# Linear attention, MoE and a second MoE on one core: four of seven VectorE steps of the first three weight conversions given to GpSimd

## The chip, the cores and the metric

The kernel runs on one core of a Trainium2 chip. The metric is the device time of one execution in microseconds (us). Five engines work side by side, each through its own list of instructions in a fixed order: TensorE multiplies matrices, VectorE (DVE in the profile) and ScalarE (ACT) work elementwise, GpSimd (POOL) can do so too, and SyncE (SP) issues the DMA transfers. An instruction that waits for another engine holds up everything behind it in its own list.

## What is computed

```
kv  = einsum('bhsd,bhse->bhde', k, v)          # attention: 4 batches, 8 heads, 576 x 64
out = einsum('bhsd,bhde->bhse', q, kv)
x   = out / sqrt(mean(out**2) + 1e-6) * g_norm # -> 2304 tokens x 512
h   = x @ w_in                                 # first MoE, 512 -> 2048 -> 512, weights float64
x   = (h * clip(h + 3, 0, 6) / 6) @ w_out
for e in range(4):                             # second MoE, experts 512 -> 1024 -> 512
    y += p[:, e] * (relu(x @ w1[e]) @ w2[e])   # p: domain_probs, normalised
```

The weights `w_in` and `w_out` of the first MoE come as float64. They are read as pairs of 32-bit words and turned on the chip into a float32 value, which is then split into a high and a low part.

## The kernel before

The attention goes in eight half batches (4 batches, 4 heads at a time). For half batch i the program does: `att_load` (three DMAs for q, k, v); `att_q` (TensorE transposes q into `pq` and `kvp`, ScalarE copies it to `qT`, L217); `att_kv` (TensorE forms k'v in `kvp`, L227; ScalarE copies it to `qT` and to `kvbd`, L232 and L234); `att_out` (TensorE multiplies `qT` with `kvbd` into `po`, L247; ScalarE squares `po`, L253; VectorE sums the squares, L256); `att_rms` (ScalarE takes a root `s`, L277; VectorE makes `va`, `r0`, `ri`, L279 to L285, and scales `po` into `xt`, L269); `att_x` (TensorE transposes `xt` into `px`, L304; ScalarE and VectorE write its high and low parts, L314 and L315). The three banks of `po` are the same for every half batch, so the matmuls of the next one wait until L269 has read them.

Beside this run the conversions of the weights. The first MoE has 16 weight tiles of 128 hidden units; a tile is a half of `w_in` (h = 0) and a half of `w_out` (h = 1). Each half takes three steps on ScalarE (Abs of the high words into `x`, L144; a copy of the low words into `r`, L145; the high part of the result `w`, L160) and seven on VectorE: the clamp of `x` (L147), the shifts of `x` (L149), the bit operations into `a` and back into `x` (L153, L155), the multiplication and addition in `r` (L157, L158), and the subtraction that gives the low part (L162). `x` and `a` have one buffer each and `r` has two, so a half can't begin on `x` before the half ahead of it has multiplied. Raw words have three buffers.

`convert` is a generator; `pull` takes steps from it against a budget of ns. The order in which each engine's instructions stand is not that of the code, though: a scheduler settles it when the program is built, out of its own idea of when each is ready. It puts the conversions of tiles 0 to 2 among the instructions of the eight half batches. Tiles 0 to 2 here are the three with n = 0, 1, 2.

After the half batches TensorE works through the first MoE (`ff_in`, `ff_out`), and then the second.

Of the kernel before, what the change touches and what calls it, by code (L numbers as in the profile page):

```python
# [8 lines left out]
F32 = mybir.dt.float32  # L9
# [3 lines left out]
ALU = mybir.AluOpType  # L13
# [4 lines left out]
def kernel(  # L18
# [18 lines left out]
    nc = tc.nc  # L37
# [20 lines left out]
    TH = 384  # L58
    FP = NF2 // 2
    NW = 8  # L60
    NA = NW - 2
    LAG = 3
    RATE = (4200, 3000, 2600, 2900, 0)
# [53 lines left out]
    def load_raw():  # L117
        if not todo:
            return
        n, h = todo.pop(0)  # L120
        u, f = ftiles[n]
        g = sum(UNITS1[:u]) + f
        r = rawp.tile([P, KD * P, 2], U32, tag="raw", name="raw")
        if h == 0:
            nc.sync.dma_start(
                out=r.rearrange("p (c f) w -> p c (f w)", c=KD),
                in_=moe_w_in.bitcast(U32)[:, 2 * g * P:2 * (g + 1) * P].rearrange("(c p) f -> p c f", p=P))
        else:
            nc.sync.dma_start(
                out=r.rearrange("p e w -> p (e w)"), in_=moe_w_out.bitcast(U32)[g * P:(g + 1) * P, :])  # L130
        raw[n, h] = r

    def convert(n):

        u, f = ftiles[n]
        W[u, f] = w = wp.tile([P, 2, 2, KD * P], F32R, tag=f"w{(NA + n) % NW}", name="w")

        for h in range(2):
            lo, hi = raw[n, h][:, :, 0], raw[n, h][:, :, 1]
            x = cvp.tile([P, KD * P], U32, tag="x", name="x")  # L140
            a = cvp.tile([P, KD * P], U32, tag="a", name="a")
            r = cvp.tile([P, KD * P], F32, tag="r", bufs=2, name="r")
            xf = x.bitcast(F32)
            nc.scalar.activation(out=xf, in_=hi.bitcast(F32), func=AF.Abs)  # L144
            nc.scalar.activation(out=r, in_=lo, func=AF.Copy, scale=2.0 ** -52)  # L145
            yield 0
            nc.vector.tensor_scalar(  # L147
                out=xf, in0=xf, scalar1=2.0 ** -15, scalar2=122880.0, op0=ALU.max, op1=ALU.min)
            nc.vector.tensor_scalar(  # L149
                out=x, in0=x, scalar1=5, scalar2=2,  # L150
                op0=ALU.logical_shift_left, op1=ALU.logical_shift_right)
            yield 670
            nc.vector.scalar_tensor_tensor(  # L153
                out=a, in0=hi, scalar=0xC0000000, in1=x, op0=ALU.bitwise_and, op1=ALU.bitwise_or)
            nc.vector.tensor_scalar(out=x, in0=a, scalar1=0xFF800000, scalar2=None, op0=ALU.bitwise_and)  # L155
            yield 940
            nc.vector.tensor_tensor(out=r, in0=r, in1=xf, op=ALU.mult)  # L157
            nc.vector.tensor_tensor(out=r, in0=r, in1=a.bitcast(F32), op=ALU.add)  # L158
            yield 1200
            nc.scalar.activation(out=w[:, h, 0], in_=r, func=AF.Copy)  # L160
            yield 0
            nc.vector.tensor_tensor(out=w[:, h, 1], in0=r, in1=w[:, h, 0].bitcast(F32), op=ALU.subtract)  # L162
            load_raw()
            yield 600

# [242 lines left out]
    def pull(n):  # L408
        while cv[0] < len(ftiles):
            i = cv[0]  # L410
            u, f = ftiles[i]
            if cv[1] is None:
                if i >= NW and last[ftiles[i - NW]] > n - LAG:
                    return
                if u and start[u - 1, 0] > n:
                    return
                cv[1] = convert(i)
            urgent = start[u, f] <= n + 1
            if budget[0] <= 0 and not urgent:
                return  # L420
            try:
                budget[0] -= next(cv[1])
            except StopIteration:
                cv[0], cv[1] = i + 1, None

    firsts = convert(0)

    def conv(k):
# [3 lines left out]

    zero = wp.tile([P, DM], mybir.dt.bfloat16, tag=f"w{NW - 1}", name="zero")
    nc.vector.memset(zero, 0.0)
# [51 lines left out]
    for n in range(NI):  # L486
        step(n)
        if n == 4 * NB:
# [6 lines left out]
                out=prob, in0=dp, in1=psum_e.unsqueeze(2).to_broadcast([P, NTT, E]), op=ALU.mult)  # L495
# [32 lines left out]
    def load2(k):  # L528
        if k >= NQ:
            return  # L530
        _, e, j = quads[k]
        raw2[k] = r = wp.tile([P, 2, 2 * KD * P], F32, tag=f"w{(NA + len(ftiles) + k % 2) % NW}", name="raw2")
        f = 2 * j * P
# [31 lines left out]
    def convert_out(k):  # L565

        r = raw2.pop(k)[:, 1].rearrange("p (f d) -> p f d", f=2)
        wout[k] = w = wp.tile(
            [P, 2, 2, DM], F32R, tag=f"w{(NA + len(ftiles) + 2 + k % 2) % NW}", name="wout")
        for f in range(2):  # L570
# [106 lines left out]
    def quad(k):  # L677
# [3 lines left out]
        g2[k] = g = [  # L681
            wp.tile([P, 2, 2, TH], F32R, tag=f"w{(NA + len(ftiles) + 4 + 2 * (k % 2) + f) % NW}", name="g2")
            for f in range(2)]
# [112 lines left out]
```

## Time and profile before

| | before |
|---|---|
| median of 3 runs | 1229.06 us (1228.98 to 1230.06) |
| profiled execution | 1228.86 us, of which the span from first to last instruction 1227.0 us |
| TensorE (PE) busy | 1206.8 us, 98% of the span |
| VectorE busy | 771.0 us, 63% |
| ScalarE busy | 586.6 us, 48% |
| GpSimd busy | 1.6 us, 13 instructions |
| granted TensorE clock | 0.999 over the span |

The chain that ended last is 93% TensorE. Busy time of TensorE is a model and overlaps itself, so 98% says that little is idle and not that all of it is at its peak. What is idle lies in the first 90 us, where the eight half batches are.

### The profile page before, as it was taken

How to read it: one execution, taken by the hardware profiler on the slowest of the kernel's cores; microseconds unless marked ns; L12 is line 12 of the kernel's file. 1: busy time of each engine (PE TensorE's matmuls, PEld its weight loads, DVE VectorE, ACT ScalarE, POOL GpSimd, SP SyncE). 2: the span in 40 equal slices, each digit the busy share in tenths (PEclk: the TensorE clock that was granted, in tenths of full speed). 3: DMA queues.
4: the chain of work that ended last, by engine and by line, in shares of the span. 5: the costliest groups of instructions: out<-in, count | busy, mean ns of one | idle time of the engine just before them, and what ended most of it. 6: DMA issues, size and time to landing. Idle time of an engine off the chain costs nothing.

```text
span 1227.0 us, 17550 instructions
## 1 busy us (share of the span) xinstructions
PE 1206.8 (98%) x7069; PEld 1061.9 (87%) x7069; DVE 771.0 (63%) x1469; ACT 586.6 (48%) x1146; POOL 1.6 (0%) x13
## 2 busy tenths in 40 slices
PE   7899999999999999999999999999999999999998
PEld 5778888888888889999999989999999899999997
DVE  5989996673522645565656585656565856565653
ACT  6778453442422434444444554444444644444442
POOL 0000000000000000000000000000000000000000
PEclk9999999999999999999999999999999999999999
DMA  8812221110100002221122132211222221111101
GB/s 338 261 58 86 70 86 35 43 44 1 37 33 1 1 1 70 69 69 69 69 70 69 69 116 73 70 69 69 69 69 69 87 92 64 65 65 63 68 32 52
DMA packets 60833, 87.15 MB, mean 71 GB/s; under 512 B 5200, under 2 KB 37968, under 8 KB 60752
## 3 DMA queue, kind: packets, MB, share of 16 engines
q1 hardware_dynamic: 60592, 86.03, 20.5%
q8 instruction: 55, 0.90, 0.3%
q14 instruction: 26, 0.21, 0.0%
q10 hardware_dynamic: 160, 0.00, 0.0%
HBM read 81.30 MB, written 4.72 MB: 70 GB/s over the span
## 4 chain that ended last, share of the span: by engine, by line
PE 93%; DVE 3%; ACT 1%; DMA 1%; issue 0%; SPq 0%
PE po L637 32%; PE po L356 16%; PE qa L663 14%; PE qb L663 14%; PE ph L333 5%; PE ph L334 5%; PE ph L335 5%; PE po L247 1%; DMA raw<-in_moe_w_out_dram 1%; DVE acc L653 1%; DVE xl L315 1%; PE px L304 0%; DVE xt L269 0%; DMA qin<-in_q_dram 0%; DVE ssq L256 0%; ACT xh L314 0%
## 5 line engine op out<-in xcount | busy, mean ns | idle before, releaser
L637 PE MATMUL po<-wout,g 128*128 128x512 f32 x1728 | 402.1, 390 | 0.0
L637 PEld LDWEIGHTS po<-wout,g 128*128 128x128 f32 x1728 | 323.6, 188 | 65.4
L663 PE MATMUL qb<-xs,win 128*128 128x384 f32 x1008 | 203.3, 336 | 1.2 <-ACT us L704 1.2
L663 PE MATMUL qa<-xs,win 128*128 128x384 f32 x1008 | 203.0, 336 | 0.0
L356 PE MATMUL po<-gH,w 128*128 128x512 f32 (+1 forms) x640 | 193.9, 368 | 0.0
L663 PEld LDWEIGHTS qb<-xs,win 128*128 128x128 f32 x1008 | 178.0, 188 | 3.8 <-ACT us L704 1.8
L663 PEld LDWEIGHTS qa<-xs,win 128*128 128x128 f32 x1008 | 178.2, 188 | 2.2 <-ACT us L704 0.2
L544 DVE TENSOR_TENSOR wout<-raw,wout 128x512 fp32r<-128x512 f32 x96 | 62.2, 688 | 171.1 <-ACT wout L543 171.1
L543 ACT ACTIVATE wout<-raw 128x512 fp32r<-128x512 f32 x96 | 55.4, 625 | 226.6 <-PE po L637 226.6
L356 PEld LDWEIGHTS po<-gH,w 128*128 128x128 f32 x640 | 117.1, 189 | 20.0
L339 ACT ACTIVATE r<-ph,three 128x512 f32<-128x512 f32 (+1 forms) x80 | 51.5, 643 | 152.8 <-PE ph L335 152.2
L333 PE MATMUL ph<-xh,w 128*128 128x512 f32 (+1 forms) x320 | 118.3, 370 | 0.1
L356 PE MATMUL po<-gL,w 128*128 128x512 f32 (+1 forms) x320 | 117.9, 369 | 0.0
L334 PE MATMUL ph<-xl,w 128*128 128x512 f32 (+1 forms) x320 | 117.8, 368 | 0.0
L335 PE MATMUL ph<-xh,w 128*128 128x512 f32 (+1 forms) x320 | 117.8, 368 | 0.0
L340 DVE SCALAR_TENSOR_TENSOR r<-r,ph 128x512 f32<-128x512 f32 (+1 forms) x80 | 50.6, 632 | 105.7 <-ACT r L339 105.5
L693 DVE SCALAR_TENSOR_TENSOR g<-sums,g 128x384 fp32r<-128x384 f32 x96 | 53.5, 558 | 81.4 <-ACT g L690 81.4
L690 ACT ACTIVATE g<-cs 128x384 fp32r<-128x384 f32 x96 | 50.4, 525 | 63.6 <-DVE cs L706 54.4
L543 ACT ACTIVATE win<-sums 128x512 fp32r<-128x512 f32 x96 | 60.7, 632 | 40.2 <-DVE sums L556 37.7
L693 DVE SCALAR_TENSOR_TENSOR g<-cs,g 128x384 fp32r<-128x384 f32 x96 | 53.3, 555 | 27.2 <-ACT g L690 27.2
L333 PEld LDWEIGHTS ph<-xh,w 128*128 128x128 f32 x320 | 60.3, 188 | 11.1 <-DVE r L340 0.6
L334 PEld LDWEIGHTS ph<-xl,w 128*128 128x128 f32 x320 | 60.3, 189 | 10.1
(95 smaller groups left out, 1258.0 us busy)
## 6 DMA issues: line engine op xcount, KB each, us to landing
raw<-in_moe_w_dram SPq DMA_DIRECT2D x96, 512.0 KB, 4.2
raw<-in_moe_w_in_dram SPq DMA_DIRECT2D x16, 512.0 KB, 3.7
raw<-in_moe_w_out_dram SPq DMA_DIRECT2D x16, 512.0 KB, 3.6
qin<-in_q_dram SPq DMA_DIRECT2D x8, 576.0 KB, 8.0
kin<-in_k_dram SPq DMA_DIRECT2D x8, 576.0 KB, 5.8
vin<-in_v_dram SPq DMA_DIRECT2D x8, 576.0 KB, 7.1
out_dram<-acc SPq DMA_DIRECT2D x18, 256.0 KB, 2.0
dp<-in_moe_domain_probs_dram SPq DMA_DIRECT2D x1, 36.0 KB, 6.4
```

The costliest lines, as they stand in the source:

```text
L333: nc.tensor.matmul(ph, lhsT=w[:, 0, c, :], rhs=xH[t][:, c, :], start=(c == 0), stop=False)
L334: nc.tensor.matmul(ph, lhsT=w[:, 0, c, :], rhs=xL[t][:, c, :], start=False, stop=False)
L335: nc.tensor.matmul(ph, lhsT=w[:, 1, c, :], rhs=xH[t][:, c, :], start=False, stop=(c == KD - 1))
L339: nc.scalar.activation(out=r, in_=ph, func=AF.Relu, bias=three[:, 0:1])
L340: nc.vector.scalar_tensor_tensor(out=r, in0=r, scalar=6.0, in1=ph, op0=ALU.min, op1=ALU.mult)
L356: nc.tensor.matmul(po_t[u, t][o], lhsT=lhsT, rhs=rhs, start=(f == 0 and m == 0), stop=(f == UF[u] - 1 and m == 2))
L543: nc.scalar.activation(out=dst[0], in_=src, func=AF.Copy)
L544: nc.vector.tensor_tensor(out=dst[1], in0=src, in1=dst[0].bitcast(F32), op=ALU.subtract)
L637: nc.tensor.matmul(ps[i], lhsT=lhsT, rhs=w[:, f, y], start=(j == 0 and f == 0 and m == 0), stop=(j == FP - 1 and f == 1 and m == 2))
L663: nc.tensor.matmul(bank, lhsT=w[:, wy, AOP[m], c], rhs=xs[m][:, xy, c], start=first and n == 0, stop=n == 5, skip_group_check=True)
L690: nc.scalar.activation(out=g[f][:, 0, t], in_=src, func=func)
L693: nc.vector.scalar_tensor_tensor(out=g[f][:, 1, t], in0=src, scalar=0.0, in1=g[f][:, 0, t].bitcast(F32), op0=ALU.max, op1=ALU.subtract)
```

## The change

For tiles 0, 1 and 2 the clamp, the multiplication, the addition and the subtraction are issued on GpSimd; the shifts and the two bit operations stay on VectorE. The budget that a step is charged is smaller for these tiles. Later tiles are as before. Two lines are added above, so from `convert` on a line number is 2 higher in the new program (L160 is L162 there, L277 is L279).

```diff
+    NPOOL = 3
...
         u, f = ftiles[n]
+        e = nc.gpsimd if n < NPOOL else nc.vector
...
-            nc.vector.tensor_scalar(
+            e.tensor_scalar(
                 out=xf, in0=xf, scalar1=2.0 ** -15, scalar2=122880.0, op0=ALU.max, op1=ALU.min)
...
-            yield 670
+            yield 670 if n >= NPOOL else 335
...
-            nc.vector.tensor_tensor(out=r, in0=r, in1=xf, op=ALU.mult)
-            nc.vector.tensor_tensor(out=r, in0=r, in1=a.bitcast(F32), op=ALU.add)
-            yield 1200
+            e.tensor_tensor(out=r, in0=r, in1=xf, op=ALU.mult)
+            e.tensor_tensor(out=r, in0=r, in1=a.bitcast(F32), op=ALU.add)
+            yield 1200 if n >= NPOOL else 0
             nc.scalar.activation(out=w[:, h, 0], in_=r, func=AF.Copy)
             yield 0
-            nc.vector.tensor_tensor(out=w[:, h, 1], in0=r, in1=w[:, h, 0].bitcast(F32), op=ALU.subtract)
+            e.tensor_tensor(out=w[:, h, 1], in0=r, in1=w[:, h, 0].bitcast(F32), op=ALU.subtract)
```

The scheduler orders all engines anew. In the rows below `x_391`, `a_392`, `r_393` and `raw_158` belong to the second half of tile 0, `x_1411`, `r_1413` and `raw_160` to the first half of tile 1, `x_1426`, `r_1428` and `raw_176` to its second half; `kvbd1_109` is here that of half batch 1 and `kvbd0_108` that of half batch 2; `w_162` and `w_1410` are the converted tiles 0 and 1.

The first place is ScalarE ahead of `kvbd` of half batch 1. Before:

```order
L217 ACTIVATE qT_306<-pq_308 128x64x8 [waits PE_49]
L144 ACTIVATE x_1411<-raw_160 128x512 [waits DVE_49]
L232 ACTIVATE qT_306<-kvp_309 128x64 [waits PE_49]
L234 ACTIVATE kvbd1_109<-kvp_309 64x64 x2
L232 ACTIVATE qT_306<-kvp_310 128x64 [waits PE_49]
L234 ACTIVATE kvbd1_109<-kvp_310 64x64 x2
L160 ACTIVATE w_162<-r_393 128x512 [waits DVE_49]
L253 ACTIVATE xt_406<-po_407 128x512 [waits PE_49]
```

Now:

```order
L219 ACTIVATE qT_306<-pq_308 128x64x8 [waits PE_49]
L146 ACTIVATE x_1411<-raw_160 128x512 [waits Pool_49]
L162 ACTIVATE w_162<-r_393 128x512 [waits Pool_49]
L234 ACTIVATE qT_306<-kvp_309 128x64 [waits PE_49]
L236 ACTIVATE kvbd1_109<-kvp_309 64x64 x2
L234 ACTIVATE qT_306<-kvp_310 128x64 [waits PE_49]
L236 ACTIVATE kvbd1_109<-kvp_310 64x64 x2
L316 ACTIVATE xh0_111<-px_430,gcol_104 128x512 [waits DMAHW7_49,DMAHW5_49,PE_49]
```

The Abs of the next half now waits for GpSimd's multiplication, and the high part of `w_162`, which stood behind `kvbd`, stands in front of it and waits for GpSimd's addition.

The second place is ScalarE ahead of `kvbd` of half batch 2. Before:

```order
L277 ACTIVATE s0_427<-ssq_110,eps4_103 128x20 [waits DVE_49]
L314 ACTIVATE xh1_112<-px_440,gcol_104 128x2x64 [waits PE_49]
L217 ACTIVATE qT_458<-pq_459 128x64x8 [waits PE_49]
L217 ACTIVATE qT_458<-pq_460 128x64x8 [waits PE_49]
L232 ACTIVATE qT_458<-kvp_461 128x64 [waits PE_49]
L234 ACTIVATE kvbd0_108<-kvp_461 64x64 x2
L232 ACTIVATE qT_458<-kvp_462 128x64 [waits PE_49]
L234 ACTIVATE kvbd0_108<-kvp_462 64x64 x2
```

Now:

```order
L255 ACTIVATE xt_406<-po_417 64x256 [waits PE_49]
L146 ACTIVATE x_1426<-raw_176 128x512 [waits Pool_49]
L316 ACTIVATE xh0_111<-px_435,gcol_104 128x512 [waits PE_49]
L279 ACTIVATE s0_427<-ssq_110,eps4_103 128x20 [waits DVE_49]
L316 ACTIVATE xh1_112<-px_440,gcol_104 128x2x64 [waits PE_49]
L162 ACTIVATE w_1410<-r_1413 128x512 [waits Pool_49]
L219 ACTIVATE qT_458<-pq_459 128x64x8 [waits PE_49]
L219 ACTIVATE qT_458<-pq_460 128x64x8 [waits PE_49]
L162 ACTIVATE w_1410<-r_1428 128x512 [waits Pool_49]
L234 ACTIVATE qT_458<-kvp_461 128x64 [waits PE_49]
L236 ACTIVATE kvbd0_108<-kvp_461 64x64 x2
```

Both halves of tile 1 have moved up: the Abs of its second half now follows the squares of half batch 1, and the high part of that half stands between the `qT` copies and `kvbd`.

The third place is VectorE in `att_rms` of half batch 1. Before:

```order
L279 TENSOR_SCALAR va_426<-ssq_110 128x20 [waits DVE_49]
L281 RECIPROCAL r0_428<-s0_427 128x20 [waits Activation_49]
L315 SCALAR_TENSOR_TENSOR xl0_116<-px_435,gcol_104,xh0_111 128x512 [waits PE_49]
L282 SCALAR_TENSOR_TENSOR va_426<-va_426,r0_428 128x20 [waits DVE_49]
L315 SCALAR_TENSOR_TENSOR xl1_117<-px_440,gcol_104,xh1_112 128x2x64 [waits Activation_49]
L284 TENSOR_TENSOR va_426<-va_426,s0_427 128x20 [waits DVE_49]
L153 SCALAR_TENSOR_TENSOR a_1412<-raw_160,x_1411 128x512 [waits DMAHW2_49]
L285 RECIPROCAL ri_429<-va_426 128x20 [waits DVE_49]
L155 TENSOR_SCALAR x_1411<-a_1412 128x512 [waits DVE_49]
L269 TENSOR_TENSOR xt_406<-po_407,ri_429 128x512 [waits DVE_49]
```

Now:

```order
L281 TENSOR_SCALAR va_426<-ssq_110 128x20 [waits DVE_49]
L151 TENSOR_SCALAR x_1426<-x_1426 128x512 [waits Pool_49]
L283 RECIPROCAL r0_428<-s0_427 128x20 [waits Activation_49]
L317 SCALAR_TENSOR_TENSOR xl0_116<-px_435,gcol_104,xh0_111 128x512 [waits PE_49]
L284 SCALAR_TENSOR_TENSOR va_426<-va_426,r0_428 128x20 [waits DVE_49]
L317 SCALAR_TENSOR_TENSOR xl1_117<-px_440,gcol_104,xh1_112 128x2x64 [waits Activation_49]
L286 TENSOR_TENSOR va_426<-va_426,s0_427 128x20 [waits DVE_49]
L155 SCALAR_TENSOR_TENSOR a_1427<-raw_176,x_1426 128x512 [waits DMAHW3_49]
L287 RECIPROCAL ri_429<-va_426 128x20 [waits DVE_49]
L157 TENSOR_SCALAR x_1426<-a_1427 128x512 [waits DVE_49]
L271 TENSOR_TENSOR xt_406<-po_407,ri_429 128x512 [waits DVE_49]
```

The shifts of tile 1's second half, one half later than what stood here before, now stand ahead of `r0` and wait for GpSimd's clamp.

## Rows read from the trace of the kernel before

**Rows 1.** Windows: stretch, its length, busy us of each engine, clock, DMA.
```profile
0.00:30.00 30.00, 21.10 (x452) 15.88 (x456) 16.61 (x39) 18.59 (x41) 1.64 (x13) 0.94 0.91 344
30.00:60.00 30.00, 26.20 (x596) 21.84 (x586) 29.41 (x74) 21.76 (x57) 0.00 (x0) 1.00 0.82 255
...
90.00:160.00 70.00, 70.00 (x338) 58.77 (x337) 67.10 (x125) 45.78 (x84) 0.00 (x0) 1.00 0.24 76
```
**Rows 2.** Chain of work that ended last: start, us, what.
```profile
6.43 10.14 DMA raw<-in_moe_w_out_dram
...
17.31 0.43 DVE x L147
...
19.48 0.64 DVE r L157
...
22.09 4.00 PE po L247 x18
...
34.81 0.60 DVE w L162
...
46.85 0.60 DVE w L162
...
51.98 0.43 DVE x L147
...
58.63 0.54 DVE r L157
```
**Rows 3.** Timeline of ScalarE, 16 to 33 us: start, us, instruction, idle before.
```profile
16.59 0.69 ACT L144 ACTIVATE x<-raw 128x512 f32<-128x512 f32 x1 [1.74 <-DMA raw<-in_moe_w_out_dram]
...
20.16 0.67 ACT L144 ACTIVATE x<-raw 128x512 f32<-128x512 f32 x1 [0.50 <-DVE r L157]
20.73 0.27 ACT L232 ACTIVATE qT<-kvp 128x64 f32<-128x64 f32 x1
...
21.59 0.45 ACT L234 ACTIVATE kvbd<-kvp 64x64 f32<-64x64 f32 x2
21.94 0.62 ACT L160 ACTIVATE w<-r 128x512 fp32r<-128x512 f32 x1
...
25.44 1.06 ACT L253 ACTIVATE xt<-po 128x512 f32<-128x512 f32 x2 [0.56 <-PE po L247]
...
31.79 0.45 ACT L234 ACTIVATE kvbd<-kvp 64x64 f32<-64x64 f32 x2
```
**Rows 4.** GpSimd's groups, shapes kept apart: busy us, mean ns of one.
```profile
masks.py:199 POOL TENSOR_SCALAR_AFFINE_SELECT ident<-ident 128x128 f32<-128x128 f32 x1 | 0.3, 292 | 0.0
...
L449 POOL MEMSET three<- 128x1 f32 x1 | 0.1, 98 | 0.0
```
**Rows 5.** VectorE's groups in the first 100 us.
```profile
L157 DVE TENSOR_TENSOR r<-r,x 128x512 f32<-128x512 f32 x9 | 6.1, 682 | 0.5 <-ACT r L145 0.3
...
L162 DVE TENSOR_TENSOR w<-r,w 128x512 fp32r<-128x512 f32 x8 | 5.5, 684 | 0.9 <-ACT w L160 0.9
```
**Rows 6.** Timeline of VectorE, 17 to 31 us.
```profile
17.77 0.43 DVE L149 TENSOR_SCALAR x<-x 128x512 uint32<-128x512 uint32 x1
...
18.97 0.43 DVE L155 TENSOR_SCALAR x<-a 128x512 uint32<-128x512 uint32 x1
...
28.21 0.28 DVE L281 RECIPROCAL r<-s 128x20 f32<-128x20 f32 x1
...
30.20 0.36 DVE L155 TENSOR_SCALAR x<-a 128x512 uint32<-128x512 uint32 x1
```
**Rows 7.** Timeline of ScalarE, 75 to 82 us.
```profile
75.55 1.14 ACT L160 ACTIVATE w<-r 128x512 fp32r<-128x512 f32 x2
...
77.54 1.23 ACT L145 ACTIVATE r<-raw 128x512 f32<-128x512 uint32 x2
...
80.43 0.45 ACT L234 ACTIVATE kvbd<-kvp 64x64 f32<-64x64 f32 x2
```
**Rows 8.** Windows of 2 us, columns as in rows 1.
```profile
22.00:24.00 2.00, 1.96 (x10) 1.91 (x10) 1.40 (x4) 0.82 (x3) 0.00 (x0) 0.54 1.04 410
```

## The prediction

> **What bounds the kernel now.** I read the table of windows first. The reader sees two different stretches in it. In the first 30 us TensorE is busy for 21.1 us and in the next 30 us for 26.2 us, so some 12.7 us are idle there [rows 1]. From 90 to 160 us it is busy for all 70 us although VectorE, at 67.1 us, is close to full [rows 1]. So the end moves only if the moment moves at which TensorE's unbroken work begins, at about 90 us; a free microsecond on VectorE after that is worth nothing. The stretch before it is a loop of waits: TensorE's `po` (L247) needs `kvbd` from ScalarE (L234) and, through the banks, VectorE's scaling of the half batch before (L269).
>
> Next I read the chain that ended last, within this stretch. Moved steps of tiles 0 to 2 stand on it six times, with 0.43, 0.64, 0.60, 0.60, 0.43 and 0.54 us, together 3.24 us [rows 2]. Last I read the timelines of ScalarE and VectorE around the places where the order changes. They show what is ready when: `raw` of tile 0's second half lands at 16.57 us (6.43 and 10.14) [rows 2], its Abs runs from 16.59 to 17.28 us, `kvbd` of half batch 1 is written from 20.73 (first L232) to 22.04 us (end of the second L234), and the high part of tile 0 comes only then, at 21.94 us [rows 3].
>
> **What the change removes and adds.** Four steps in each of six halves leave VectorE: 0.43 us for a clamp [rows 2] and about 0.68 us for each of the three others [rows 5], so 6 x 2.47 = 14.8 us, of which the 3.24 us above are on the chain. GpSimd gets 24 instructions. It had 13 short ones, so it is free; what they last there the trace does not show.
>
> Its nearest rows: one instruction that reads and writes 128 x 128 takes 0.292 us, and one with a single column 0.098 us [rows 4]. Four times the columns give (0.292 - 0.098) x 4 + 0.098 = 0.87 us for the clamp, with one input. With two inputs read one after the other this becomes 0.776 x 2 + 0.098 = 1.65 us. The lower end is VectorE's own time, 0.43 and 0.68 us. I take 0.87 us for the clamp, since that row is the nearest, and the middle, 1.2 us, for the steps with two inputs; an estimate. The Trainium skill has a figure for the latter (GPSIMD Engine Reference, 3.1 Elementwise): 4497 ns for a `tensor_tensor` add of 2048 fp32 elements, by which 512 would take an estimated 1.1 us, and the sum below would be 0.3 us smaller. No run here shows it yet.
>
> **Place 1, `kvbd` of half batch 1.** ScalarE now has the Abs of the next half and then the high part of tile 0 in front of `kvbd`, and the latter waits for GpSimd's addition. What is queued behind it: both `kvbd` writes, which `po` of half batch 1 waits for, and with it the squares and everything after. The chain, from rows:
> - Abs ends 17.28 [rows 3]; clamp on GpSimd 0.87: 18.15.
> - Shifts to the last bit operation on VectorE, with the small steps of `att_rms` between them: 17.77 to 19.40 before, so 1.63 [rows 6]: 19.78.
> - Multiplication and addition on GpSimd, 2.4: 22.18. The Abs of the next half fits beside the addition.
> - High part on ScalarE 0.62, then 1.31 for the four writes (20.73 to 22.04) [rows 3]: 24.11. Five handoffs at 0.03 (17.28 to 17.31 [rows 2, 3]) add 0.15: 24.26.
>
> It was 22.04, so half batch 1 is 2.2 us late. With VectorE's durations it would be 0.7 us, with 1.65 us 3.1 us. The scaling of half batch 0, freed of three steps, ends earlier, but is no longer the last to arrive. The same exchange ahead of `kvbd` of half batch 0 costs nothing: what follows there waits for `raw`, which lands at 16.57 us however late that `kvbd` is by up to a microsecond.
>
> **Place 2, `kvbd` of half batch 2.** Here the whole second half of tile 1 has moved in front.
> - `po`: 18 matmuls take 4.00 [rows 2], at a clock of 0.54 [rows 8], from 24.26: 28.26. The last square ends 0.41 later (26.50 against 26.09 before) [rows 2, 3]: 28.67.
> - Abs 0.67 [rows 3]: 29.34. Clamp 0.87: 30.21.
> - Shifts 0.43 [rows 6], which now stand ahead of `r0` on VectorE, so that the root's chain waits for them: 30.64. From there to the end of the last bit operation 2.35 (28.21 to 30.56 before) [rows 6]: 32.99.
> - Multiplication and addition 2.4, high part 0.62, four writes 1.31, six handoffs 0.18: 37.5.
>
> Before, it was 32.24 us (31.79 and 0.45) [rows 3]. So half batch 2 is 5.2 us late; with the lower durations 2.3 us, with the upper 7.1 us.
>
> **What is given back, and place 3.** From here on the loop is as before with less on VectorE. Of the six pieces on the chain three lie later, 0.60, 0.43 and 0.54 us [rows 2]; I let them go in full, 1.6 us, since what comes last then is the next step of the same chain of `att_rms`. The bit operations that stay cost there what they cost before. Place 3 is tile 2's end: its `w` shares a buffer with `qT`, so its high parts come at 75.55 us, behind half batch 6. In the new order a copy of low words (L145) that needs GpSimd's first subtraction stands in front of the `qT` copies of half batch 7. The first high part ends near 76.12, the subtraction 1.2 later; ScalarE, done with the second at 76.69 [rows 7], idles for 0.7 us with the `qT` copies and `kvbd` (until 80.88 before [rows 7]) behind it. With the ends of the range this is 0.1 and 1.1 us.
>
> SyncE's queue changes by one place: a raw load of tile 3 goes behind k, v and q of half batch 6. Nothing waits for tile 3 before half batch 7; at worst its loss is that of place 3. GpSimd's own queue carries no DMA.
>
> **The sum.** 5.2 - 1.6 + 0.7 = 4.3 us later at the start of TensorE's unbroken work, which then takes as long as before. The profiled execution took 1228.86 us, so 1233.2; the median of the runs is 0.2 us above the profiled one, so 1233.4 us. The likeliest case's own range: 2.3 - 1.6 + 0.1 = 0.8 us gives 1229.9; 7.1 - 1.6 + 1.1 = 6.6 us, and up to 1.8 us if the low clock that `po` of half batch 1 meets (4.00 us at 0.54 would be about 2.2 at full clock) also falls on half batch 2, gives 1237.5.
>
> **Rivals.**
> - Faster: the relief of VectorE decides, and no wait takes its place. All 3.24 us on the chain go: 1225.8 us. For it speaks VectorE's 29.4 busy us out of 30 between 30 and 60 us [rows 1]. It decides if GpSimd's addition at place 1 is done by about 20.1 us, so that `kvbd` is not held; against it, the last bit operation ends at 19.8 us, and even VectorE would need 1.36 us for the two steps behind it. 12 in 100.
> - No change: GpSimd runs near VectorE's speed and the later half batches give the rest back, 0.8 us of loss or less, 1229 to 1230 us. For it speaks that ScalarE, too, has fewer conversion steps in half batches 4 to 6, now that tile 1 is done earlier. 20 in 100.
> - Slower still: VectorE and GpSimd hinder each other. The subtraction of tile 1's first half runs beside the root's steps of half batch 1 (place 2), and the multiplication of tile 2's first half beside those of half batch 2; if a VectorE step with two inputs waits out a whole GpSimd step, 1.2 us come on top at each: 1235.8 us. The trace has no two such steps side by side. The Trainium skill states it as a rule (SBUF — State Buffer, Who interferes with whom): a VectorE instruction with two SBUF inputs, or in a two-port mode, and a GpSimd instruction that reads SBUF exclude each other for a whole instruction. By that rule 1235.8 us would stand in place of 1233.4, wherever the two meet as worked out; no run here shows it yet. 20 in 100.
>
> **How the numbers follow.** The forecast has the remaining 48 in 100. A measurement of this kernel can tell about 0.2%, 2.5 us, from no change, so slower means above 1231.5 us: most of the forecast's chance and the third rival's, 0.65; within, the second rival and the forecast's low end, 0.23; faster, 0.12. The range for 8 in 10 leaves out the faster rival and little at the top: 1228 to 1238 us.
>
> **What would show it.** In the changed profile ScalarE idles in front of the high part (L162) at about 21 to 22 us and again before 35 us, released by GpSimd's addition (L160), and `kvbd` of half batch 2 ends near 37.5 us; VectorE's shifts (L151) wait for GpSimd's clamp near 30 us. `kvbd` of half batch 7 ends 4 to 5 us later than 80.88 us [rows 7], and after 95 us nothing of TensorE differs. The forecast is wrong if GpSimd's steps take 0.7 us or less, if ScalarE does not idle there, or if half batches 3 to 7 take more than 2 us less than before.

## The result, and the profile after

The changed kernel takes 1244.12 us (median of 4 runs, 1242.33 to 1246.67); the kernel before took 1229.56 us beside it. The ratio is 1.0117, 95% interval 1.0096 to 1.0139, so the change makes the kernel 14.6 us slower. The forecast was 1233.4 us, its range 1228 to 1238 us: the direction was right, the size was not. The profiled execution took 1242.33 us, 13.5 us more than that of before, and its span is 1240.5 us. It is the fastest of the four, at a granted clock of 0.992 over the span; the other three had 0.989, 0.989 and 0.986 and took 1243.78 to 1246.67 us. What is read from the trace below accounts for the 13.5 us; what makes up the difference to the median was not looked into.

The windows of the changed kernel (stretch, its length, busy us and instructions of TensorE, its weight loads, VectorE, ScalarE and GpSimd, clock, DMA):

```profile
0.00:30.00 30.00, 19.77 (x341) 14.41 (x342) 10.89 (x23) 15.63 (x35) 14.91 (x22) 0.84 0.92 343
30.00:60.00 30.00, 22.74 (x508) 18.85 (x508) 21.10 (x51) 17.98 (x48) 13.91 (x10) 0.94 0.49 143
...
90.00:160.00 70.00, 67.81 (x328) 56.53 (x329) 64.61 (x124) 46.77 (x91) 0.00 (x0) 0.98 0.25 76
```

VectorE got 14.0 us freer in the first 60 us (46.02 in [rows 1], 31.99 now), and TensorE lost 4.8 us there (47.30 and 42.51). So the time set free on VectorE did not reach TensorE.

GpSimd's groups, shapes kept apart (busy us, mean ns of one, then its idle time and what ended it):

```profile
L149 POOL TENSOR_SCALAR x<-x 128x512 f32<-128x512 f32 x6 | 11.5, 1916 | 18.9 <-ACT x L146 18.9
L160 POOL TENSOR_TENSOR r<-r,a 128x512 f32<-128x512 f32 x6 | 8.0, 1327 | 0.5
L159 POOL TENSOR_TENSOR r<-r,x 128x512 f32<-128x512 f32 x6 | 7.6, 1270 | 12.4 <-DVE x L157 10.6 <-DVE va L286 1.8
L164 POOL TENSOR_TENSOR w<-r,w 128x512 fp32r<-128x512 f32 x6 | 7.6, 1266 | 21.1 <-ACT w L162 21.1
```

The steps with two inputs take 1.27 to 1.33 us, near the 1.2 of the forecast (the 1.33 of the addition is a mean that contains one of 1.62). The clamp, with one input, takes 1.92 us, 4.5 times VectorE's 0.43, where [rows 4] had led to 0.87.

The clearest reading of where the time goes is the end of the second `kvbd` write of each half batch, in ScalarE's timeline:

| end of `kvbd`, us | 0 | 1 | 2 | 3 | 4 | 5 | 6 | 7 | whole run |
|---|---|---|---|---|---|---|---|---|---|
| before | 12.20 | 22.04 | 32.24 | 40.32 | 51.38 | 61.09 | 69.34 | 80.88 | 1228.86 |
| after | 13.88 | 26.74 | 42.93 | 50.47 | 60.12 | 71.91 | 80.21 | 92.97 | 1242.33 |
| later by | 1.7 | 4.7 | 10.7 | 10.2 | 8.7 | 10.8 | 10.9 | 12.1 | 13.5 |

Places 1 and 2 in ScalarE's timeline after (start, us, instruction, idle before and what ended it), against [rows 3]:

```profile
17.76 0.68 ACT L146 ACTIVATE x<-raw 128x512 f32<-128x512 f32 x1
...
24.89 0.63 ACT L162 ACTIVATE w<-r 128x512 fp32r<-128x512 f32 x1 [0.68 <-POOL r L160]
...
26.29 0.45 ACT L236 ACTIVATE kvbd<-kvp 64x64 f32<-64x64 f32 x2
...
31.36 0.68 ACT L146 ACTIVATE x<-raw 128x512 f32<-128x512 f32 x1 [0.22 <-POOL r L159]
...
41.07 0.63 ACT L162 ACTIVATE w<-r 128x512 fp32r<-128x512 f32 x1 [6.50 <-POOL r L160]
...
42.48 0.45 ACT L236 ACTIVATE kvbd<-kvp 64x64 f32<-64x64 f32 x2
```

ScalarE stands idle for 6.50 us in front of the high part of tile 1, with `kvbd` of half batch 2 right behind it. What it waits for, in GpSimd's timeline:

```profile
31.40 1.28 POOL L160 TENSOR_TENSOR r<-r,a 128x512 f32<-128x512 f32 x1
32.65 1.91 POOL L149 TENSOR_SCALAR x<-x 128x512 f32<-128x512 f32 x1
34.53 1.26 POOL L164 TENSOR_TENSOR w<-r,w 128x512 fp32r<-128x512 f32 x1
38.41 1.28 POOL L159 TENSOR_TENSOR r<-r,x 128x512 f32<-128x512 f32 x1 [2.62 <-DVE x L157]
```

and in VectorE's, against [rows 6], with two later stretches that are needed below:

```profile
34.59 1.48 DVE L151 TENSOR_SCALAR x<-x 128x512 uint32<-128x512 uint32 x1 [1.88 <-POOL x L149]
...
62.71 0.43 DVE L151 TENSOR_SCALAR x<-x 128x512 uint32<-128x512 uint32 x1 [2.28 <-POOL x L149]
...
64.24 0.68 DVE L342 SCALAR_TENSOR_TENSOR r<-r,ph 128x512 f32<-128x512 f32 x1
...
87.16 1.23 DVE L284 SCALAR_TENSOR_TENSOR va<-va,r 128x20 f32<-128x20 f32 x1
88.42 1.20 DVE L286 TENSOR_TENSOR va<-va,s 128x20 f32<-128x20 f32 x1
```

Look at the durations, not only at the idle times. The shifts at 34.59 us last 1.48 us, not 0.43; the two steps on 128x20 at 87 us last 1.23 and 1.20 us, where their like before lasts 0.17. Each ends within 0.3 us after a GpSimd subtraction does: the shifts at 36.07, 0.28 us after 34.53 + 1.26 = 35.79, and the two steps at 88.39 and 89.62, beside two subtractions of 1.25 us each that run from 87.08 to 89.58. So these look like waits that the profile books as work; the run with the prices below tests it.

### The profile page after: what moved, and what is told of

It is laid out like the page before. It is cut to its first block, busy times and chain, and to the rows that moved or that the text cites. A ratio compares the mean times of both kernels' runs of the same rounds, so it can differ in the third digit from the quotient of the medians.

```text
span 1240.5 us, 17562 instructions
## 1 busy us (share of the span) xinstructions
PE 1211.9 (98%) x7069; PEld 1066.3 (86%) x7069; DVE 765.2 (62%) x1445; ACT 587.3 (47%) x1146; POOL 36.1 (3%) x37
## 4 chain that ended last, share of the span: by engine, by line
PE 93%; DVE 3%; POOL 1%; ACT 1%; issue 0%; DMA 0%; DVEq 0%; POOLq 0%
PE po L639 31%; PE po L358 16%; PE qa L665 14%; PE qb L665 14%; PE ph L336 5%; PE ph L335 5%; PE ph L337 5%; PE po L249 1%; POOL x L149 1%; DVE acc L655 1%; DVE xl L317 1%; PE px L306 0%; POOL r L159 0%; DVE x L151 0%; DMA raw<-in_moe_w_in_dram 0%
## 5 line engine op out<-in xcount | busy, mean ns | idle before, releaser
L342 DVE SCALAR_TENSOR_TENSOR r<-r,ph 128x512 f32<-128x512 f32 (+1 forms) x80 | 50.6, 632 | 106.6 <-ACT r L341 106.4
```

The costliest lines, as they stand in the source:

```text
L342: nc.vector.scalar_tensor_tensor(out=r, in0=r, scalar=6.0, in1=ph, op0=ALU.min, op1=ALU.mult)
```

## The experiments

The theories: **size** (the clamp's 1.92 us carries the excess), **order** (a conversion step ahead of `kvbd` on ScalarE does the harm, whatever its length), **shared access** (VectorE and GpSimd hold each other up), and **latency at every place** (wherever attention's work is queued behind a conversion step, that half's whole chain is paid for; nothing is given back for good). In the edits `e` is split into `ec` (clamp), `em` (multiplication and addition) and `es` (subtraction), and G stands for `nc.gpsimd if n < NPOOL else nc.vector`. Two things go along with each edit. The scheduler orders every program anew. And the runs that start from the changed kernel keep its smaller budgets in `pull`, also for steps that are back on VectorE; a run with these budgets alone was not made. The run with tile 2 alone, below, bounds what they do: its tiles 0 and 1 have the small budgets and all their steps on VectorE, and up to half batch 3 it is at most 0.4 us later than before. In the run with tile 0 alone, tiles 1 and 2 are like that, and nothing more is lost from half batch 3 on.

**Which steps.** The clamp back on VectorE, and the clamp alone on GpSimd:

```diff
-        e = G
+        ec, em, es = nc.vector, G, G
```

> The clamp of the three tiles goes back to VectorE; multiplication, addition and last subtraction stay on GpSimd. Theory size (the clamp's 1.92 us on GpSimd against 0.43 on VectorE carries the excess): the chain up to kvbd of half batch 2 holds four clamps, 4 x 1.49 = 6.0 us come back, about 1238. Theory order (the conversion to the high part stands ahead of kvbd on ScalarE and holds it until GpSimd is done, whatever the clamp costs): that place in the order stays, so kvbd of half batch 1 and 2 stay late; only the clamps that stand in the chain itself shorten, 1 or 2 of them, 1241 to 1243. A middle result would say that the two add up.

```diff
-        e = G
+        ec, em, es = G, nc.vector, nc.vector
```

> Only the clamp of the three tiles runs on GpSimd, all else on VectorE. On ScalarE the conversions to the high part then stand behind kvbd of half batch 1 as before, one Abs stands ahead of kvbd of half batch 2. Theory size: the four clamps of the chain cost 4 x 1.49 = 6 us, about 1235. Theory order: next to nothing, 1229 to 1231, since what waits for the clamp stands behind kvbd. Both would have the shift on VectorE wait about 1.5 us for each clamp.

Measured: 1236.85 us (ratio to before 1.0057, 1.0042 to 1.0072) and 1234.66 us (1.0040, 1.0025 to 1.0055). Taking the clamp back returns 7.3 us, putting it there alone costs 5.0 us. Size said 1238 and 1235, order 1241 to 1243 and 1229 to 1231: order alone is out. Size met both times, but it is a theory of the excess over the forecast: half of the whole loss remains without the clamp, and size does not say where that comes from.

The subtraction alone, multiplication and addition alone, and the changed kernel with the subtraction back:

```diff
-        e = G
+        ec, em, es = nc.vector, nc.vector, G
```

> Only the last subtraction of the three tiles runs on GpSimd (1.27 us against 0.69). Nothing of attention waits for its result before half batch 4. Theory latency (only steps that something in a queue waits for cost): 1229 to 1230, or up to 1 us faster, since VectorE loses 6 x 0.69 = 4.1 us of work. Theory shared access (VectorE's small instructions of the normalisation are held while a subtraction runs, about 1 us each time): 1231 to 1233.

```diff
-        e = G
+        ec, em, es = nc.vector, G, nc.vector
```

> Only multiplication and addition of the three tiles run on GpSimd (1.27 us each against 0.69). The conversion to the high part again stands ahead of kvbd of half batch 1 on ScalarE. The run with the clamp back on VectorE lost 7.1 us. Theory latency: all of that is from multiplication and addition, 1235 to 1237. Theory shared access: part of it came from the subtractions on GpSimd that held VectorE, 1232 to 1234.

```diff
-        e = G
+        ec, em, es = G, G, nc.vector
```

> The changed kernel with the last subtraction of the three tiles back on VectorE; clamp, multiplication and addition stay on GpSimd. Theory additive (each group of steps costs its own latency: clamp 5.0, multiplication and addition 5.5, subtraction 3.2, together 13.7 of the 14.4 measured): 3 us come back, 1240 to 1242. Theory shared access as the main cost (what holds VectorE is the subtraction on GpSimd, at five places for 1.0 to 1.1 us each): 5 us or more come back, 1239 or less. Theory queue only: the subtraction is behind nearly everything, 1243 to 1245.

Measured: 1233.37 us (1.0023, 1.0014 to 1.0033), 1235.68 us (1.0046, 1.0031 to 1.0061), 1240.11 us (1.0080, 1.0065 to 1.0095). Above the kernel before as it was timed beside each, the three parts cost 5.0, 5.5 and 3.2 us, together 13.7 of 14.6, so within their intervals they add (the clamp, which returned 7.3 us when it was taken back, is the least sure). Multiplication and addition came out as the latency theory of their run said, 1235 to 1237. I had held it possible that the subtraction costs nothing, since no attention step waits for its result before half batch 4. It costs 3.2 us all the same, about what shared access had said (1231 to 1233). VectorE's timeline in that run shows two ways how: shifts that last 1.46 and 1.44 us and not 0.43, and two tiny steps in half batch 7:

```profile
22.72 1.46 DVE L151 TENSOR_SCALAR x<-x 128x512 uint32<-128x512 uint32 x1
...
34.69 1.44 DVE L151 TENSOR_SCALAR x<-x 128x512 uint32<-128x512 uint32 x1
...
78.28 1.24 DVE L284 SCALAR_TENSOR_TENSOR va<-va,r 128x20 f32<-128x20 f32 x1
79.55 1.20 DVE L286 TENSOR_TENSOR va<-va,s 128x20 f32<-128x20 f32 x1
80.78 0.28 DVE L287 RECIPROCAL ri<-va 128x20 f32<-128x20 f32 x1
```

Two subtractions of 1.25 us run on GpSimd from 78.21 us, and VectorE's two tiny steps, all that is left to do before `ri`, wait out one each. Before, VectorE did both subtractions and both tiny steps here in 1.38 us; now it is 2.50. With the subtraction back on VectorE (the third run) no shift is held; this view gives the shortest, median and longest duration in ns of one line, here the shifts of that run:

```profile
L151 DVE TENSOR_SCALAR x<-x x32: 355/427/429, 7.6 to 338.2; 128x512 uint32<-128x512 uint32 x32
```

In the changed kernel the longest is 1480. The time that comes back, 4.0 us by the medians (4.5 by the ratios), lies between the additive theory's 3 and the 5 or more of shared access as the main cost; the time itself is in the additive theory's range, 1240 to 1242.

**The prices by themselves.** The kernel before, with GpSimd instructions on 128x512 added behind its work, first alone, then beside VectorE instructions started by the same event:

```diff
+    for g, v, m in (
+            (g_two, None, 0), (g_clamp, None, 0), (g_single, None, 0),
+            (g_two, v_small, 4), (g_clamp, v_small, 4), (g_two, v_tiny, 4), (g_two, v_scalar, 3),
+            (g_two, v_reduce, 3), (g_two, v_psum, 3), (g_clamp, v_psum, 3)):
+        trigger()
+        g()
+        for _ in range(m):
+            v()
```

> The kernel before with work added behind it that changes no output: single GpSimd instructions on 128x512 float32 in SBUF (addition of two inputs; clamp with two constants; maximum with one constant), first with VectorE idle, then beside VectorE instructions started by the same event: 128x20 maximum of two inputs, 128x20 with constants, 128x512 with constants, a 128x512 reduction, and a 128x384 maximum with one input in PSUM. Theory shared access (VectorE and GpSimd exclude each other for some forms): alone 1.27 and 1.92; beside them one of VectorE's forms is stretched to the end of GpSimd's instruction (0.16 becomes 1.1 to 1.9), and GpSimd's own durations stay. Theory of long prices alone: all durations are the same beside and alone. For the maximum with one constant: if the price goes by the number of operations, about 1.0; if it goes by the form, 1.9.

Measured on GpSimd: 1.26 to 1.29 us for an addition (1.50 for one, below), 1.92 us for two clamps and 2.16 for the first, 1.50 us for the maximum with one constant. So the maximum with one constant lies between the two answers that I had put down, 1.0 and 1.9. VectorE's lines (shortest, median and longest ns), maximum of two inputs, with constants on 128x20, with constants on 128x512:

```profile
L786 DVE TENSOR_TENSOR sums<-sums x8: 169/179/1132, 1226.3 to 1233.7; 128x20 f32<-128x20 f32 x8
L792 DVE TENSOR_SCALAR sums<-sums x4: 176/176/1132, 1235.5 to 1237.1; 128x20 f32<-128x20 f32 x4
L789 DVE TENSOR_SCALAR sums<-sums x3: 426/426/1368, 1238.1 to 1239.9; 128x512 f32<-128x512 f32 x3
```

and its groups with the reduction and with an input in PSUM (busy us, mean ns of one):

```profile
L799 DVE TENSOR_TENSOR sums<-qa,sums 128x384 f32<-128x384 f32 x6 | 3.3, 557 | 0.2
...
L795 DVE TENSOR_REDUCE sums<-sums 128x8 f32<-128x512 f32 x3 | 2.0, 682 | 0.0
```

Shared access is real and selective: of the first three forms one instruction each is held for some 0.95 us by GpSimd's two-input addition; reductions and steps that read PSUM aren't. GpSimd's clamp holds too, but only in its first third. Beside the clamp of this run (from 1232.79 to 1234.71 us) the second of the four maxima on 128x20 lasts 0.48 us and not 0.18, and ends 0.64 us after the clamp began; the two behind it take their usual time:

```profile
1232.95 0.48 DVE L786 TENSOR_TENSOR sums<-sums 128x20 f32<-128x20 f32 x1
```

The changed kernel has the same, and there the held step ends 0.64 us after the clamp's start as well:

```profile
18.53 1.92 POOL L149 TENSOR_SCALAR x<-x 128x512 f32<-128x512 f32 x1 [4.53 <-ACT x L146]
18.57 0.60 DVE L281 TENSOR_SCALAR va<-ssq 128x20 f32<-128x20 f32 x1
```

Later inside a clamp VectorE is free: in the run with the clamp alone it adds two inputs in its usual time, starting 0.67 us into a clamp that runs from 33.43 to 35.34 us:

```profile
34.10 0.67 DVE L160 TENSOR_TENSOR r<-r,a 128x512 f32<-128x512 f32 x1
```

The Trainium skill (SBUF — State Buffer, Who interferes with whom) says that a VectorE instruction with two SBUF inputs contends with a GpSimd instruction that reads SBUF. The two-input rows agree (1132 against 179 beside the addition, 0.48 us against 0.18 beside the clamp). But the whole instruction, by which the third rival reckoned, is not waited out beside the clamp: there the measurement decides, 0.64 of 1.92 us.

**Which places.** In the next two runs the order on ScalarE is held near that of before; in the second also for tile 3. `behind(step, i)` tells the scheduler to put the step behind the last `kvbd` write of half batch i in ScalarE's list, with no wait of its own:

```diff
             wh = nc.scalar.activation(out=w[:, h, 0], in_=r, func=AF.Copy)
+            behind(wh, {(0, 1): 1, (1, 0): 2, (1, 1): 3}.get((n, h)))   # (tile, half): kvbd of half batch
...
             ab = nc.scalar.activation(out=xf, in_=hi.bitcast(F32), func=AF.Abs)
+            behind(ab, {(1, 1): 2}.get((n, h)))
```

> All four steps on GpSimd as in the changed kernel, but the order on ScalarE is held near that of before: the conversion to the high part of tile 0's second half stays behind kvbd of half batch 1, tile 1's first half and the Abs of its second half behind kvbd of half batch 2. Theory order: kvbd of half batch 1 ends within 2 us and that of half batch 2 within 4 us of before (22.0 and 32.2), and the time is 1232 to 1236. Theory size: the steps of the conversion themselves are late wherever they stand, VectorE's shifts wait for the clamp and hold what stands behind them, and the time stays at 1241 to 1244.

```diff
-            behind(ab, {(1, 1): 2}.get((n, h)))
+            behind(ab, {(1, 1): 2, (3, 0): 5, (3, 1): 7}.get((n, h)))
             lc = nc.scalar.activation(out=r, in_=lo, func=AF.Copy, scale=2.0 ** -52)
+            behind(lc, {(3, 0): 7, (3, 1): 7}.get((n, h)))
```

> As the run with the order held (all four steps on GpSimd), and besides on ScalarE the Abs of tile 3's first half stays behind kvbd of half batch 5, and tile 3's other ScalarE steps behind kvbd of half batch 7. Theory order (the loss is made only where ScalarE meets a conversion step ahead of kvbd): kvbd of half batch 5 comes back from 72.2 to about 67.5, and the time to 1236 to 1239. Theory latency in every queue (VectorE's shift, which waits 3 us for the clamp at 60 us, stands ahead of attention's work there too): kvbd of half batch 5 comes back by 2 us at most, 1240 to 1243.

All four steps for tile 2 only, and for tile 0 only:

```diff
-        e = G
+        e = nc.gpsimd if n == 2 else nc.vector
```

> All four steps on GpSimd, for tile 2 only; tiles 0 and 1 stay on VectorE, so nothing can be late before about 50 us. Theory early places (the loss is made at kvbd of half batches 1 and 2 and merely carried through half batches 3 to 6, as the changed kernel's steady lateness of 10.5 to 10.8 suggests): tile 2 adds the step at half batch 7 alone, 1.2 us and its low clock, 1230 to 1232. Theory every place (wherever a conversion on GpSimd stands ahead of attention's work in a queue, its whole latency is lost there; in the run with the order held, 5 us were lost at half batch 5): 1234 to 1237.

```diff
-        e = G
+        e = nc.gpsimd if n == 0 else nc.vector
```

> All four steps on GpSimd, for tile 0 only. Place 1 then costs what it cost in the changed kernel (kvbd of half batch 1 4.7 us late), place 2 only what tile 0 hands on. Theory carried: half batches 2 to 7 give nothing back, 1233.5 to 1235. Theory given back: the later chains have the slack that the prediction counted on (0.60, 0.43, 0.54), 1231 to 1233.

The ends of `kvbd` in their profiles, later than before by, in us (the last run below, which changes nothing ahead of half batch 5, also differs there by up to 0.3 us):

| run | median us (ratio to before) | 1 | 2 | 3 | 4 | 5 | 6 | 7 |
|---|---|---|---|---|---|---|---|---|
| order held | 1242.78 (1.0114, 1.0097 to 1.0132) | 3.1 | 3.5 | 5.4 | 5.9 | 11.1 | 10.9 | 12.1 |
| order held, tile 3 too | 1240.10 (1.0080, 1.0066 to 1.0094) | 3.5 | 4.0 | 5.8 | 5.5 | 8.3 | 8.5 | 6.8 |
| tile 2 alone | 1235.45 (1.0043, 1.0027 to 1.0060) | 0.4 | 0.4 | 0.4 | 1.2 | 3.6 | 3.4 | 4.6 |
| tile 0 alone | 1234.31 (1.0038, 1.0023 to 1.0053) | 5.0 | 5.8 | 6.9 | 6.8 | 6.3 | 6.2 | 6.2 |

Holding the order takes 7.2 us out of place 2, as the order theory said (3.5 late and not 10.7), though half batch 1 stays 3.1 us late and not within its 2. The end hardly moves: the order theory's 1232 to 1236 us is out, the 1241 to 1244 of size came, and 5.2 us are lost at half batch 5 in its stead. ScalarE there:

```profile
62.90 0.68 ACT L154 ACTIVATE x<-raw 128x512 f32<-128x512 f32 x1 [1.83 <-POOL r L168]
63.49 0.62 ACT L354 ACTIVATE gH<-r 128x512 fp32r<-128x512 f32 x1
```

The Abs of tile 3's first half waits for GpSimd's multiplication of tile 2 (they share the buffer `x`), with attention's work behind it. With that one moved as well the whole gains 2.7 us more by the medians (4.2 by the ratios) and is still 9 us behind the kernel before. Neither expectation was met in full: `kvbd` of half batch 5 comes back by 2.8 us, more than the 2 of latency in every queue and far less than the 4.7 of order, and the time is in the range of the former. Its `kvbd` of half batch 7 ends at 87.71 us, but `po` there starts only at 89.86. In tile 2's run nothing is later than 0.4 us up to half batch 3, and 5.3 us are lost all the same; its VectorE and its ScalarE show the same two kinds of wait:

```profile
55.27 0.43 DVE L151 TENSOR_SCALAR x<-x 128x512 uint32<-128x512 uint32 x1 [3.05 <-POOL x L149]
```

```profile
62.65 0.68 ACT L146 ACTIVATE x<-raw 128x512 f32<-128x512 f32 x1 [2.33 <-POOL r L159]
```

Tile 0's run loses 5 us at place 1, and half batches 2 to 7 give none of it back; its median of 1234.31 us is what "carried" said (the profiled execution, at 1236.66, is its slowest). So either of the two tiles costs 4 to 5 us by itself, at its own place; tile 1 was not run alone. Latency at every place stands; the theory of tile 2's run that the loss is made early, at half batches 1 and 2, and only carried on is out.

**Conversion steps behind `kvbd` in the kernel before.** If any conversion step ahead of `kvbd` costs its time, the kernel before has some of that too: at half batch 7 ScalarE's copies and Abs of tile 3 stand in front of it [rows 7]. All conversions stay on VectorE in these two runs:

```diff
+            behind(ab, {(1, 0): 1, (3, 0): 5, (3, 1): 7}.get((n, h)))
+            behind(lc, {(3, 0): 7, (3, 1): 7}.get((n, h)))
```

> The kernel before (all conversions on VectorE), with four places of ScalarE's order changed: the Abs of tile 1's first half behind kvbd of half batch 1, that of tile 3's first half behind kvbd of half batch 5, tile 3's last three steps behind kvbd of half batch 7. If any conversion step that stands ahead of kvbd costs its time there: 0.6 at half batch 1, 0.3 at 5, 0.9 to 1.5 at 7, of which tile 3 gives some back later, 1228 to 1229. If the conversions themselves then come late and are waited for elsewhere: 1230 to 1232.

```diff
-            behind(ab, {(1, 0): 1, (3, 0): 5, (3, 1): 7}.get((n, h)))
+            behind(ab, {(3, 0): 5, (3, 1): 7}.get((n, h)))
```

> The kernel before with ScalarE's order changed only for tile 3: the Abs of its first half behind kvbd of half batch 5, its last three steps behind kvbd of half batch 7. In the run with four places changed, kvbd of half batch 1 came 1.2 us earlier, but that of half batch 2 0.8 later, so the place at half batch 1 seems to cost 0.8 net; half batches 5 and 7 gave 0.2 and 1.7. If places add: kvbd of half batch 2 as before (32.2), that of half batch 7 at about 79.1, 1.8 earlier than before, and the time 1227 to 1229. If what half batch 7 gains is lost again behind it, since tile 3 is converted later: kvbd as said, the time within 0.5 us of before.

Measured: 1228.42 us against 1231.14 (ratio 0.9980, 0.9971 to 0.9989), and 1228.63 us against 1229.82 (0.9990, 0.9981 to 0.9999), 11 runs each. Both are a little faster than the kernel before, by 2.7 and 1.2 us. The second is only just clear of no difference, and its interval doesn't exclude the other theory's 0.5 us. In the second, `kvbd` of half batch 2 ends at 32.11 us, that of half batch 7 at 79.31, 1.6 us earlier than before, as expected. In ScalarE's timeline the copies of low words now stand behind it:

```profile
78.86 0.45 ACT L246 ACTIVATE kvbd<-kvp 64x64 f32<-64x64 f32 x2
79.21 1.22 ACT L156 ACTIVATE r<-raw 128x512 f32<-128x512 uint32 x2
```

Whether the first place (tile 1's Abs behind `kvbd` of half batch 1) helps or hurts stays open: the two runs were not made on the same chip side by side.

## Why the prediction was wrong, step by step

- **What bounds the kernel: right.** VectorE lost 14 us of work in the first 60 us and the end came later. That the late start carries to the end held too.
- **The clamp's price: wrong, 0.87 against 1.92 us.** It was scaled from an instruction with another operation [rows 4]. The 1.2 us of the two-input steps was close (1.27 to 1.33).
- **Place 1: right mechanism, 26.74 us against 24.26.** Of the 2.5 us too little, 1.05 are the clamp; 1.2 are the Abs, which starts at 17.76 us and not at 16.59. The sentence that a late `kvbd` of half batch 0 costs nothing failed: it came 1.7 us late, more than the microsecond allowed, and `po` behind it lasted 4.28 us and not 2.96. Together that is more than the 1.74 us that ScalarE had idled in front of this Abs [rows 3], and now the Abs follows the last square without a wait for `raw`. TensorE, busy for only 0.84 us from 12 to 14 us, is granted 0.50 in the next two, the lower of its two levels (1.2 GHz), where the kernel before had 1.00:

```profile
14.00:16.00 2.00, 2.00 (x11) 2.00 (x10) 0.00 (x0) 0.38 (x1) 0.00 (x1) 0.50 0.98 356
```

- **Place 2: right mechanism, 10.7 us late against 5.2.** From `kvbd` to `kvbd` it took 16.19 us and not 13.24. The 2.9 us more: the clamp 1.04; the shifts held by GpSimd's subtraction 1.05 (1.48 against 0.43); GpSimd busy with the other half's addition when the clamp was due, 0.61 (the Abs ends at 32.04, the clamp starts at 32.65); the Abs itself waiting for GpSimd's multiplication, 0.2 (0.22 us idle at 31.36). The last square ends 4.40 us after `kvbd` of half batch 1, as reckoned (4.41).
- **Given back, 1.6 us: right, and then lost.** Lateness falls from 10.7 to 8.7 us by half batch 4. Half batch 5 then takes 2.1 us back: the shifts of tile 2's second half wait 2.28 us for the clamp at 62.71 us, and `r` of the first MoE (L342) stands behind them, which ScalarE waits for (1.74 us ahead of L343) with squares of attention behind it. That place is missing in the prediction: I looked for new waits at three places, and from there on held the loop to be as before. Tile 2 alone was to cost 0.7 us in it, and costs 5.3.
- **Place 3: 1.2 us against 0.7,** by another wait than the one named: the two steps of `att_rms` held by the subtractions (1.23 and 1.20 us). ScalarE's wait for the subtraction (0.86 us ahead of L147) is there, but behind the `qT` copies ScalarE waits once more, for VectorE's multiplication of tile 3, which stands behind the held steps, so that the hold comes last:

```profile
90.51 0.66 ACT L146 ACTIVATE x<-raw 128x512 f32<-128x512 f32 x1 [0.48 <-DVE r L159]
```

- **"After 95 us nothing differs": wrong by 1.4 us.** In the changed kernel TensorE, busy for only 1.32 us from 88 to 92 us, is granted 0.59 in the next 4, that is mostly the lower of its two levels (1.2 GHz), and the last `po` of attention falls there:

```profile
92.00:96.00 4.00, 3.76 (x19) 3.64 (x20) 2.65 (x5) 1.75 (x6) 0.00 (x0) 0.59 0.12 34
```

Its 20 matmuls last 4.07 us; in the run with the subtraction back on VectorE 18 of them last 2.41.

The terms close: 4.3 us predicted, and 2.5 (place 1), 2.9 (place 2), 2.1 (half batch 5) less 0.35 (given back), 0.5 (place 3) and 1.4 (clock) make 13.4; the profiles differ by 13.5. They are differences along one row of end times, so that they must close; the split within a place is read from one execution, and no run tests it term by term.

Which steps failed, then: of the 9.1 us that are missing, 5.4 belong to places 1 and 2, whose chains were the right ones with terms too small or put at nothing. The clamp was to take 0.87 us and took 1.92, twice (2.1); the late `kvbd` of half batch 0 was put at nothing (1.2); the hold of the shifts stood only in a rival (1.05); GpSimd's own queue was put at nothing (0.6); some 0.4 are small terms. The sentence "From here on the loop is as before with less on VectorE" failed outright: 2.1 us at half batch 5. The rest is the hold at place 3 (0.5) and the clock behind attention (1.4), less the 0.35 given back.

The rivals: faster and no change are out. Slower still was right about the hold and nearly about its price (1.05 us for 1.2), and as forecast it is met at place 2, though there it is the shifts that are held, with one input, and not a step of the root with two. It gave 1235.8 us: the hold is one part of the surplus and not the whole. Of the signs named beforehand ScalarE's idle time in front of L162, the shifts' wait for the clamp and the direction came true, the first two some 3 to 6 us later than named; `kvbd` of half batch 2 was to end near 37.5 us and ends at 42.93, that of half batch 7 was to be 4 to 5 us late and is 12.1.

The run with the subtraction back shows how one place's gain is lost at the next: its `kvbd` of half batch 2 ends at 39.38 us, 3.6 earlier than in the changed kernel, and that of half batch 3 at 50.55, no earlier. There VectorE's shifts of tile 2's first half stand ahead of `r0` of half batch 2 and wait for GpSimd's clamp; in the changed kernel they stand behind it (`r0` at 47.56 us, the shifts at 47.74):

```profile
46.19 0.43 DVE L151 TENSOR_SCALAR x<-x 128x512 uint32<-128x512 uint32 x1 [1.88 <-POOL x L149]
```

`po` of half batch 2 also lasts 4.45 us there, against 2.96. How much each of the two takes was not tried.

## What to carry to other kernels

Moving work off a busy engine pays only if that engine is waited for; where a loop of handoffs sets the pace, count latency: the durations of every step in the chain on the slower engine, at every place where an in-order queue has other work behind it. Look for the cost of such a move once for each piece moved, not only where the order visibly changes, since holding the order moved the loss to the next place. The gain, a small one of 1 to 3 us, lay the other way: to put side work behind the step that the loop waits for.

## What the runs showed of the hardware

- On GpSimd a clamp of 128x512 float32 with two constants takes 1.92 us and a maximum with one constant 1.50, both longer than an addition of two such tensors (1.26).
- A GpSimd instruction with two inputs in SBUF holds VectorE instructions of three forms until it ends, even on 128x20, and VectorE's wait shows as a longer duration (up to 1.48 us for 0.43), not as idle time. A GpSimd clamp of 1.92 us holds VectorE only until 0.64 us after its start (0.48 us for 0.18 on 128x20); a two-input addition that VectorE began 0.67 us into a clamp took its usual 0.67 us.
- It works the other way as well: GpSimd's addition that started 0.05 us behind VectorE's 128x512 step with constants lasted 1.50 us and not 1.26.
